# A list-scheduled attention-plus-MLP kernel: an order found by a search over its planner's keys, a warm-up on a constant, and an earlier release of one weight load

## Chip, cores, metric

The kernel runs on one core of a Trainium2 chip. The metric is the device time in microseconds (us) of one execution; medians of several executions are given. The span in a profile is about 1.7 us shorter than the time. All runs told here were in the fast state. By the 2% rule every kernel in this document is "the same" as the one before; what is compared below lies under 2%, and the 95% intervals say which of it is clear of the scatter.

## The reference, cut to what matters

```python
x = A_x                                             # 2048 x 512
g = sigmoid((x * gate_w).sum(-1))                   # one gate per row
a = A(x)   # q, k, v = x wq, x wk, x wv; 32 heads of 16; 4 segments of 512 rows:
           # o = gb * (phi(q) M) / (phi(q) z + 1e-6) + (1 - gb) * softmax(q k^T / 4 + mask) v
           # M += phi(k)^T v ; z += sum phi(k)    (after each segment);  a = o wo
b = B(x)   # h = relu(x W_gate) * (x W_up)  (1792 wide);  b = h W_down
out = g * a + (1 - g) * b                           # bf16
```

## The kernel before

The kernel doesn't fix an order by hand. It lists 1346 operations, each with the engines that can run it, a length in us, a key and what it depends on. A planner in the kernel then goes through simulated time and takes, on each engine, the ready operation with the lowest key. The result is the order in which all instructions are emitted. On the chip each engine is handed its own instructions in that order. Where an operand isn't there yet, the engine waits with it: at 105 us of the changed kernel, shown below, VectorE stands for 2.23 us before an operation although the operand of the next one has been ready for 1.4 us.

```python
MM, SW, MG = 0.216, 0.1, 1.0      # a dense matmul of 512 columns, a change of shape, a margin
...
    def run(self):                # in Sched
        ...
                    def pk(x):    # TensorE's choice: the key, and a bonus for staying in shape
                        t, o = x
                        k = o.key
                        if o.mode == "P":
                            k += -20.0 if mode == "R" else 4.0
                        elif o.mode == "D" and mode == "C" and "C" not in o.flex:
                            k += 3.0
                        return (k, o.seq)
        ...
            if e == "PE":
                o.ran = mode if mode in o.flex else o.mode
                if o.ran != mode:
                    dur += SW
                    mode = o.ran
```

The four shapes: D dense 128x128, C column strips 128x32, R the logits (four row strips of 32), P probabilities times values (64x32). The start, where x, wq and wk are loaded:

```python
    def c_zero(e):
        nc.vector.memset(zero[:, 0:P], 1.0)              # operand of the warm-up
    def c_dummy(e):
        for _ in range(28):                              # TensorE warm-up
            nc.tensor.matmul(g_dummy.t[:, 0:P], lhsT=zero[:, 0:P], rhs=zero[:, 0:P], ...)
    ...
    # x of segment 0 in four pieces by the SP and ACT queues; wq in three pieces by GpSimd's queue:
            nc.gpsimd.dma_start(out=wq_sb[:, c0:c1, :], in_=A_wq[c0 * P:c1 * P, :]...)
    ...
    lw["wk"] = loadw("wk", wk_sb, A_wk, 0, D, 1)         # by the SP queue; wv, wg, wu ... behind it
    o_wk0 = op("wk0", {"DVE": 0.08}, lambda e: nc.vector.memset(wk_sb[0:1, 0, 0:1], 0.0), key=-490, cls=0)
    lw["wk"].deps.append((o_wk0, None))
    ...
    o_wk0.deps.append((xc0[0][0], None))                 # after the first copy of x
```

The memset of one element of wk_sb is there only so that the load of wk has to wait for it. In the body, three things matter later: VectorE empties the PSUM of k and v (PSUM holds the buffers that TensorE writes its results to), it multiplies RG out of R, which GpSimd copies together, and it transposes output tiles that GpSimd has summed.

```python
            nc.gpsimd.tensor_copy(R[s][32 * j:32 * j + 32, k, :], rcol[32 * k:32 * k + 32, cols])  # 16 a segment
            nc.vector.tensor_tensor(RG[s % 2]..., HG..., rv..., ALU.mult)             # op RG{s}, waits for all R
            (nc.vector if e == "DVE" else nc.gpsimd).tensor_tensor(Oa.t[:], Oa.t[:], Ob.t[:], ALU.add)  # ad{s}{c}
            nc.vector.transpose(dst.t[:], Oa.t[:]...)                                 # ot{s}{c}, waits for ad
```

Of the kernel before, what the change touches and what calls it, by code (L numbers as in the profile page):

```python
# [7 lines left out]
BF16 = mybir.dt.bfloat16  # L8
F32 = mybir.dt.float32
ACT = mybir.ActivationFunctionType  # L10
ALU = mybir.AluOpType

P = 128
# [12 lines left out]
VW = H * HP + 16  # L26
VSW = H // 2 * HP + 16

MM = 0.216
SW = 0.1  # L30
MG = 1.0



# [20 lines left out]
class Sched:  # L55
# [5 lines left out]
    def op(self, name, engs, emit, deps=(), key=0.0, cls=1, mode=None, alloc=(), uses=(), land=0.0, flex=""):  # L61
        o = Op()
        o.flex, o.ran = flex, mode
        o.name, o.engs, o.emit, o.key, o.cls, o.mode = name, engs, emit, key, cls, mode
        o.alloc, o.uses = list(alloc), list(alloc) + list(uses)
        o.deps = [d if isinstance(d, tuple) else (d, None) for d in deps]
        o.deps = [d for d in o.deps if d[0] is not None]
        o.start = o.end = o.eng = None
        o.land = land
        o.succ, o.seq = [], len(self.ops)  # L70
        for b in o.uses:
            b.left += 1
        self.ops.append(o)
        return o
# [92 lines left out]
def kernel(  # L167
# [15 lines left out]
    nc = tc.nc  # L183
# [6 lines left out]
    def tl(name, shape, dt=BF16):  # L190
        return sb.tile(list(shape), dt, name=name)
# [9 lines left out]
    wq_sb, wk_sb, wv_sb, wo_sb = (tl(n, [P, NC, D]) for n in ("wq_sb", "wk_sb", "wv_sb", "wo_sb"))  # L201
# [1 line left out]
    ident = tl("ident", [P, P])  # L203
    mcol = tl("mcol", [P, 1], F32)
    mcole = tl("mcole", [P, 1], F32)
    scratch = tl("scratch", [P, 1], F32)
    bdm = tl("bdm", [P, 8, DH], F32)
    mzacc = tl("mzacc", [P, NC, 2 * (DH + 1)], F32)
    M2 = [tl(f"M2_{i}", [P, NC, 8, DH]) for i in range(2)]
# [13 lines left out]
    Op_ = pool("O", 4, [P, 16, 2, DH])  # L223
    oTp = pool("oT", 8, [P, L])
    osp = rgp = pool("os", 4, [P, D])
    zero = osp.tiles[0]
    smp = pool("sm", 3, [P, 2, 16], F32)
    zg, zc, rcol, rp1, ngcol = (tl(n, [P, NT], F32) for n in ("zg", "zc", "rcol", "rp1", "ngcol"))
    R = [tl(f"R{s}", [P, 4, 4], F32) for s in range(NSEG)]
# [8 lines left out]
    sc = Sched()  # L238
    op = sc.op
# [9 lines left out]
    ACTC = lambda n: 0.19 + 0.000833 * n  # L249


    def c_zero(e):
        nc.vector.memset(zero[:, 0:P], 1.0)  # L253
    o_zero = op("zero", {"DVE": 0.15}, c_zero, cls=0, key=-100)

    def c_ident(e):
        nc.gpsimd.memset(ident[:], 0.0)
# [2 lines left out]
    o_ident = op("ident", {"POOL": 0.6}, c_ident, cls=0, key=-100)  # L260

    def c_warm(e):
        nc.scalar.activation(scratch[:], zero[:, 0:1], ACT.Exp)
    o_warm = op("warm", {"ACT": 1.5}, c_warm, deps=[o_zero], cls=0, key=-100)

    def c_mcol(e):
# [20 lines left out]
    o_bdm = op("bdm", {"POOL": 1.5}, c_bdm, deps=[o_ident, o_vones], key=-10)  # L287

    def c_dummy(e):
        for _ in range(28):  # L290
            nc.tensor.matmul(g_dummy.t[:, 0:P], lhsT=zero[:, 0:P], rhs=zero[:, 0:P], start=True, stop=True)  # L291
    g_dummy = Buf(G)
    o_dummy = op("dummy", {"PE": 3.0}, c_dummy, deps=[o_zero], key=-1000, mode="D", alloc=[g_dummy])

# [18 lines left out]
    for i in range(2):  # L313
        for eng, q, h in (("SP", nc.sync, 0), ("ACT", nc.scalar, 1)):
            def f(e, i=i, q=q, h=h):
                q.dma_start(out=xn[0].t[:, 2 * h:2 * h + 2, 256 * i:256 * i + 256],
                            in_=x[256 * h:256 * h + 256, 256 * i:256 * i + 256].rearrange("(t p) d -> p t d", p=P))
            lx0[i, h] = load(f"x0_{i}{h}", f, 131072, -300 + i, eng=eng, alloc=[xn[0]] if (i, h) == (0, 0) else [],
                             uses=[] if (i, h) == (0, 0) else [xn[0]])
# [12 lines left out]
        return load(name, f, P * tile_.shape[1] * (c1 - c0) * 2, key, eng=eng)  # L332

    lw["wk"] = loadw("wk", wk_sb, A_wk, 0, D, 1)
    o_wk0 = op("wk0", {"DVE": 0.08}, lambda e: nc.vector.memset(wk_sb[0:1, 0, 0:1], 0.0), key=-490, cls=0)
    lw["wk"].deps.append((o_wk0, None))
    lw["wv"] = loadw("wv", wv_sb, A_wv, 0, D, 1)

# [59 lines left out]
    qS = Buf(Spool)  # L398
# [3 lines left out]
    first_x(1, None)  # L402
    for ci in range(NC):
        def f(e, ci=ci):
            for c in range(NC):
                nc.tensor.matmul(qS.t[:, c, :], lhsT=wq_sb[:, ci, c * P:(c + 1) * P], rhs=xT[0].t[:, ci, :],  # L406
                                 start=(ci == 0), stop=(ci == NC - 1))
        o_q0 = op(f"q0.{ci}", {"PE": 4 * MM * (1.5 if ci < 2 else 1)}, f,
                  deps=xc0[ci] + lwq[ci] + [(o_q0, 0.0) if ci else None],
                  key=-400 + ci, mode="D", alloc=[qS] + q0 if ci == 0 else [], uses=([] if ci == 0 else [qS]) + [xT[0]])  # L410
        if ci < 2:
            first_x(ci + 2, o_q0)
# [193 lines left out]
    def mz_mm(s, g):  # L606
        for c in range(NC):
            for t in range(4):
                for j in range(4):
                    h = 8 * c + 2 * j  # L610
                    nc.tensor.matmul(g.t[32 * j:32 * j + 32, W2 * c:W2 * c + W2],  # L611
                                     lhsT=pK[s].t[:, t, c * P + 32 * j:c * P + 32 * j + 32],
                                     rhs=Vp[s].t[:, t, h * HP:(h + 2) * HP].rearrange("p (h v) -> p h v", v=HP)[:, :, 0:DH + 1],
                                     start=(t == 0), stop=(t == 3), tile_position=(0, 32 * j))

    def mz_deps(s):
        return [o_pKt[s, c] for c in range(NC)] + [o_v[s, t] for t in range(4)]
# [21 lines left out]
    def mz0():  # L639
        g = Buf(G)  # L640
        k = dkey(3)
        a = op("mz0", {"PE": 0.5}, lambda e: mz_mm(0, g), deps=mz_deps(0), key=k, mode="C", alloc=[g], uses=[pK[0], Vp[0]])
        mz_after(0, a, g, k)


# [69 lines left out]
    rec_of = {}  # L715
# [4 lines left out]
    def unit(i):  # L720
        s, c = units[i]
        base = TA0 + (i // 2) * 2 * PU
        odd = i % 2
        FL = [[(c, 0, 0, 512)], [(c, 1, 0, 448), (c, 7, 448, 64)], [(c, 2, 0, 384), (c, 6, 384, 128)],
              [(c, 3, 0, 320), (c, 5, 320, 192)]]
        if not odd:
            FL.append([(c, 4, 0, 256), (c + 1, 4, 256, 256)])
        E, masks = {}, []
        for n, parts in enumerate(FL):
            sp, eb_ = Buf(Spool), Buf(Ep)  # L730
            kf = base + (n + 5 * odd) * 2 * PU / 9
            chunks = sorted({p[0] for p in parts})

            def f(e, parts=parts, sp=sp):
                for cc, kb, off, w in parts:
                    for j in range(4):
                        rows = slice(32 * j, 32 * j + 32)
                        nc.tensor.matmul(sp.t[:, j, off:off + w],  # L738
                                         lhsT=K2[s, cc].t[rows, kb, :, :].rearrange("p r k -> p (r k)"),
                                         rhs=QT[s, cc].t[rows, L - w:L], start=True, stop=True,  # L740
                                         tile_position=(32 * j, 0))
            a = op(f"f{s}{c}.{n}", {"PE": MM}, f,
                   deps=[o_q[s, cc] for cc in chunks] + [o for cc in chunks for o in o_k2[s, cc]] +
                   ([(fill_prev[0], 0.0)] if fill_prev[0] else []),
                   key=kf, mode="R", alloc=[sp], uses=[b_ for cc in chunks for b_ in (QT[s, cc], K2[s, cc])])
            fill_prev[0] = a
            if n == 1 and pending[0] is not None:
                rest(*pending[0], a)
                pending[0] = None

            def f(e, sp=sp, eb_=eb_):
                nc.scalar.activation(eb_.t[:], sp.t[:], ACT.Exp, scale=SCALE)  # L752
            b = op(f"e{s}{c}.{n}", {"ACT": 1.88}, f, deps=[a], key=kf, cls=0, alloc=[eb_], uses=[sp])
            offs = [p[2] for p in parts]

            def f(e, eb_=eb_, offs=offs):
                for off in offs:
                    for r in range(2):
                        v = eb_.t[64 * r:64 * r + 64, :, off:off + 64]
                        nc.gpsimd.affine_select(out=v, in_=v, compare_op=ALU.is_ge, fill=0.0, base=0,  # L760
                                                pattern=[[0, 4], [1, 64]], channel_multiplier=-1)
            m = op(f"m{s}{c}.{n}", {"POOL": 0.95 * len(parts)}, f, deps=[b], key=kf, uses=[eb_])
            for cc, kb, off, w in parts:
                if cc == c:
                    E[kb] = (eb_, off)
                else:
                    shared[s, cc] = (eb_, off, m)
            masks.append(m)
        if odd:
            E[4] = shared[s, c][0:2]  # L770
            masks.append(shared[s, c][2])
        pending[0] = (i, E, masks)
        if i == len(units) - 1:
            rest(i, E, masks, None)
# [4 lines left out]
    def dens(s, k0, org):  # L779
# [11 lines left out]
        rec_of[s, "den"] = rec_of[s, "mz"] = a  # L791
        if mds:
            gm = Buf(G)
            rec_of[s, "mz"] = am = op(f"mz{s}", {"PE": 0.5}, lambda e: mz_mm(s, gm), deps=[(a, 0.0)], key=k0 - 20, mode="C",
                                      alloc=[gm], uses=[pK[s], Vp[s]])
            gate_mz.append((s, am, gm, k0))
        T = Buf(Tp)
# [33 lines left out]
    def rest(i, E, masks, behind):  # L831
# [4 lines left out]
        def f(e):  # L836
            for kb in range(8):
                src, off = E[kb]
                w = L - 64 * kb
                for r in range(2):  # L840
                    rows = slice(64 * r, 64 * r + 64)
                    for j in range(4):
# [3 lines left out]
                        else:  # L846
# [1 line left out]
                            v = VS[s].t[rows, kb // 2, h * HP:h * HP + 32]  # L848
                        nc.tensor.matmul(gs[r].t[32 * j:32 * j + 32, L - w:L], lhsT=v, rhs=src.t[rows, j, off:off + w],  # L849
                                         start=(kb == 0), stop=(kb == 7), tile_position=(64 * r, 32 * j))  # L850
        a = op(f"pv{s}{c}", {"PE": 1.05}, f,
               deps=[(m, MG) for m in masks] + [o_v[s, t] for t in range(4)] + [o for t in range(4) for o in o_vs[s, t]] +
               ([(behind, 0.0)] if behind else []),
               key=k0 - 100, mode="P", alloc=gs, uses=list({id(v[0]): v[0] for v in E.values()}.values()) + [Vp[s], VS[s]])
# [128 lines left out]
    for t in range(4):  # L983
        dn(NSEG - 1, t)

    order = sc.run()
    if SIM_HOOK is not None:
        SIM_HOOK(sc)
# [36 lines left out]
```

## Time and profile before

| | before |
|---|---|
| time, median of 3 | 267.07 us (266.61 to 267.48) |
| TensorE busy | 97% of a span of 265.3 us |
| first q matmul, first k matmul | 5.19 us, 9.60 us |
| changes of TensorE's shape after 9 us | 170, 95.6 ns each |
| end of the last matmul, tail after it | 262.13 us, 3.14 us |

A line of the timeline is: start, length, engine, line of the program, operation, out<-in, shapes, how many were merged, and in brackets the idle time before and what ended it. The prediction below shows the lines. "Body" is used here for the time from the start of the first k matmul to the end of the last matmul: 252.53 us. The same matmuls lie between these two points in all of the kernels compared here.

### The profile page before, as it was taken

To read this page: it belongs to the slowest core of one execution; us is meant where nothing else is said; L and a number is where in the kernel's file an instruction comes from. 1 tells how busy PE (TensorE), PEld (TensorE's weight loads), DVE (VectorE), ACT (ScalarE), POOL (GpSimd) and SP (SyncE) were. 2 spreads that over 40 slices of the span, in tenths; PEclk is the share of its full clock that TensorE was granted. 3 is DMA by queue.
4 is the path that set the end of the run, shared out by engine and by line. 5 is a ranking of instruction groups with operands and counts; after the bars stand their busy time and mean duration, and the time that the engine had idled before them with its cause. 6 is when DMAs were issued, how large, how long until landed. Compare 5 with 4: busy or idle time off the path is not lost.

```text
span 265.3 us, 7048 instructions
## 1 busy us (share of the span) xinstructions
PE 257.0 (97%) x2808; PEld 115.9 (44%) x2844; DVE 183.8 (69%) x407; ACT 193.9 (73%) x189; POOL 191.0 (72%) x470
## 2 busy tenths in 40 slices
PE   8999999999999999999999999999999999999995
PEld 6433444444454444444434434344443444344444
DVE  1497888888975285998888837688985735566611
ACT  3598999899885558999896668898788566777010
POOL 8678888888559788798648988887878866537000
PEclk9999999999999999999999999999999999999999
DMA  5997990017310100000551010000000010000011
GB/s 162 289 252 203 313 261 13 4 40 80 100 26 1 42 20 22 0 2 2 132 88 23 21 42 20 4 2 0 2 0 4 0 42 23 20 2 0 2 41 40
DMA packets 27057, 15.54 MB, mean 59 GB/s; under 512 B 13584, under 2 KB 26896, under 8 KB 27024
## 3 DMA queue, kind: packets, MB, share of 16 engines
q1 hardware_dynamic: 26304, 14.30, 22.0%
q0 software_dynamic: 176, 0.52, 0.6%
q8 instruction: 22, 0.36, 0.6%
q10 hardware_dynamic: 544, 0.26, 0.3%
q14 instruction: 11, 0.09, 0.1%
HBM read 9.84 MB, written 2.10 MB: 45 GB/s over the span
## 4 chain that ended last, share of the span: by engine, by line
PE 97%; issue 2%; DVE 0%; ACT 0%; DVEq 0%
PE G L248 74%; PE S L738 9%; PE G L849 7%; PE G L246 3%; PE S L406 2%; PE G L291 1%; PE G L611 1%; PE G L785 0%; PE G L385 0%; DVE os L700 0%; ACT xT L395 0%; DVE os L253 0%; DVE mcole L268 0%; DVEq L700 0%; DVE mcol L267 0%
## 5 line engine op out<-in xcount | busy, mean ns | idle before, releaser
L752 ACT ACTIVATE E<-S 128x2048 bf16<-128x2048 f32 x72 | 135.1, 1876 | 34.3 <-PE S L738 31.9
L760 POOL TENSOR_SCALAR_AFFINE_SELECT E<-E 64x256 bf16<-64x256 bf16 x256 | 115.7, 452 | 38.5 <-ACT E L752 24.6
L248 PE MATMUL G<-xT,wu_sb 128*128 128x512 bf16 x211 | 57.3, 380 | 0.4 <-issue 0.2
L248 PE MATMUL G<-xT,wg_sb 128*128 128x512 bf16 x206 | 56.2, 380 | 1.1 <-issue 0.8
L663 DVE TENSOR_TENSOR hT<-G,os 128x512 bf16<-128x512 f32 x56 | 38.2, 684 | 19.7 <-ACT os L659 10.7
L248 PE MATMUL G<-wd_sb,hT 128*128 128x512 bf16 (+1 forms) x212 | 48.9, 365 | 1.1 <-issue 1.0
L884 DVE STREAM_TRANSPOSE T<-G 128x512 f32<-128x512 f32 x44 | 30.3, 702 | 14.0 <-PE G L849 8.2
L659 ACT ACTIVATE os<-G 128x512 bf16<-128x512 f32 x56 | 32.7, 597 | 6.1 <-PE G L248 5.3
L248 PEld LDWEIGHTS <-wu_sb 128*128 128x128 bf16 x218 | 19.9, 98 | 24.8 <-issue 3.0
L248 PEld LDWEIGHTS <-wg_sb 128*128 128x128 bf16 x218 | 19.4, 98 | 24.6 <-issue 4.1
L248 PEld LDWEIGHTS <-hT 128*128 128x128 bf16 x222 | 20.3, 98 | 22.3 <-issue 2.6
L738 PE MATMUL S<-QT,K 32*128 32x192 bf16 (+7 forms) x512 | 28.6, 287 | 0.5
L738 PEld LDWEIGHTS <-K 32*128 32x128 bf16 x512 | 8.2, 92 | 30.4 <-issue 29.9
L700 DVE TENSOR_SCALAR os<-G,ngcol 128x512 bf16<-128x512 f32 (+1 forms) x10 | 7.0, 697 | 19.4 <-PE G L248 19.3
L849 PE MATMUL G<-E,Vp 64*32 64x128 bf16 (+7 forms) x512 | 19.0, 284 | 0.2 <-issue 0.2
L849 PE MATMUL G<-E,VS 64*32 64x128 bf16 (+7 forms) x512 | 18.4, 284 | 0.0
L248 PE MATMUL G<-wo_sb,oT 128*128 128x512 bf16 (+1 forms) x66 | 17.2, 367 | 0.3 <-issue 0.3
L597 POOL COPY VS<-Vp 64x256 bf16<-64x256 bf16 x32 | 13.3, 416 | 4.8 <-DVE Vp L515 3.3
L904 DVE TENSOR_TENSOR O<-T,sm 128x256 bf16<-128x256 f32 x32 | 15.8, 524 | 0.3
L248 PE MATMUL G<-xT,wk_sb 128*128 128x512 bf16 x60 | 15.8, 380 | 0.3 <-issue 0.2
L702 ACT ACTIVATE os<-G,ngcol 128x512 bf16<-128x512 f32 x7 | 4.8, 687 | 15.0 <-PE G L248 15.0
L479 POOL COPY R<-rcol 32x4 f32<-32x4 f32 x64 | 13.5, 210 | 3.0
(98 smaller groups left out, 302.0 us busy)
## 6 DMA issues: line engine op xcount, KB each, us to landing
out_dram<-os SPq DMA_DIRECT2D x15, 128.0 KB, 1.7
wd_sb<-in_B_W_down_dram SPq DMA_DIRECT2D x1, 1792.0 KB, 13.4
xn<-in_A_x_dram SPq DMA_DIRECT2D x3, 512.0 KB, 4.7
wg_sb<-in_B_W_gate_dram SPq DMA_DIRECT2D x2, 512.0 KB, 5.8
wu_sb<-in_B_W_up_dram SPq DMA_DIRECT2D x2, 512.0 KB, 6.9
wg_sb<-in_B_W_gate_dram SPq DMA_DIRECT2D x3, 256.0 KB, 6.9
wu_sb<-in_B_W_up_dram SPq DMA_DIRECT2D x3, 256.0 KB, 7.2
wk_sb<-in_A_wk_dram SPq DMA_DIRECT2D x1, 512.0 KB, 4.0
```

The source lines that it names most:

```text
L246: nc.tensor.matmul(out_ap[q], lhsT=lhsT[:, q], rhs=rhs, start=start, stop=stop, tile_position=(0, 32 * j))
L248: nc.tensor.matmul(out_ap, lhsT=lhsT, rhs=rhs, start=start, stop=stop)
L479: nc.gpsimd.tensor_copy(R[s][32 * j:32 * j + 32, k, :], rcol[32 * k:32 * k + 32, cols])
L597: nc.gpsimd.tensor_copy(VS[s].t[64 * r:64 * r + 64, t, 0:H // 2 * HP].rearrange("p (h v) -> p h v", v=HP)[:, :, 0:DH], src[:, :, r, 0:DH])
L659: nc.scalar.activation(rg.t[:], g.t[:], ACT.Relu)
L663: nc.vector.tensor_tensor(h.t[:], u.t[:], rg.t[:], ALU.mult)
L738: nc.tensor.matmul(sp.t[:, j, off:off + w], lhsT=K2[s, cc].t[rows, kb, :, :].rearrange("p r k -> p (r k)"), rhs=QT[s, cc].t[rows, L - w:L] ...
L752: nc.scalar.activation(eb_.t[:], sp.t[:], ACT.Exp, scale=SCALE)
L760: nc.gpsimd.affine_select(out=v, in_=v, compare_op=ALU.is_ge, fill=0.0, base=0, pattern=[[0, 4], [1, 64]], channel_multiplier=-1)
L849: nc.tensor.matmul(gs[r].t[32 * j:32 * j + 32, L - w:L], lhsT=v, rhs=src.t[rows, j, off:off + w], start=(kb == 0), stop=(kb == 7), tile_po ...
L884: nc.vector.transpose(T.t[:].rearrange("p b e -> p (b e)"), g.t[:])
L904: nc.vector.tensor_tensor(O.t[:, :, r, :], T.t[:, :, 0:DH], sm.t[:, r, :, None].to_broadcast([P, 16, DH]), ALU.mult)
```

## The change

The intent: a search over the planner's keys, with lengths corrected from measurements, looks for an order that ends sooner; the warm-up no longer waits for VectorE; wk comes sooner.

```diff
-MM = 0.216
-SW = 0.1
+MM = 0.2159
+SW = 0.094
+NUDGE = { "f13.3": 24, "q12/0": -7, "g0.0/1": 81, ... }        # 64 entries, cut
...
-    def c_zero(e):
-        nc.vector.memset(zero[:, 0:P], 1.0)
+    ones = nc.const_aps.tensor(1.0, [P, P], BF16)
...
-        nc.scalar.activation(scratch[:], zero[:, 0:1], ACT.Exp)
+        nc.scalar.activation(wk_sb[:, 0, 0:1], ones[:, 0:1], ACT.Exp)
...
-        for _ in range(28):
-            nc.tensor.matmul(g_dummy.t[:, 0:P], lhsT=zero[:, 0:P], rhs=zero[:, 0:P], start=True, stop=True)
+        for _ in range(31):
+            nc.tensor.matmul(g_dummy.t[:, 0:P], lhsT=ones, rhs=ones, start=True, stop=True)
...
-    o_wk0 = op("wk0", {"DVE": 0.08}, lambda e: nc.vector.memset(wk_sb[0:1, 0, 0:1], 0.0), key=-490, cls=0)
+    o_wk0 = op("wk0", {"DVE": 0.08}, lambda e: None, key=-490, cls=0)
...
+            if ci == 0:                                   # ahead of the first q group
+                for _ in range(2):
+                    nc.tensor.matmul(qS.t[:, 0, 0:P], lhsT=ones, rhs=ones, start=True, stop=True)
...
-        a = op("mz0", {"PE": 0.5}, ...                    # also mz{s}
+        a = op("mz0", {"PE": 0.56}, ...
-            a = op(f"f{s}{c}.{n}", {"PE": MM}, f,         # logits
+            a = op(f"f{s}{c}.{n}", {"PE": 0.229}, f,
-        a = op(f"pv{s}{c}", {"PE": 1.05}, f,              # probabilities times values
+        a = op(f"pv{s}{c}", {"PE": 1.015}, f,
...
+    for o in sc.ops:
+        o.key += NUDGE.get(o.name, 0)
     order = sc.run()
```

Note that the planner still counts the load of wk as held by the first copy of x (the operation wk0 stays in the plan); only on the chip is it released sooner, by ScalarE's warm-up, which now writes into wk_sb.

> **What bounds the kernel now.** I read the page's head first (busy shares and the 40 slices), then the waits of TensorE, then TensorE's timeline at the start and in the middle, last the end of the run.
>
> ```profile
> PE 257.0 (97%) x2808; PEld 115.9 (44%) x2844; DVE 183.8 (69%) x407; ACT 193.9 (73%) x189; POOL 191.0 (72%) x470
> ...
> PE   8999999999999999999999999999999999999995
> ...
> PE 97%; issue 2%; DVE 0%; ACT 0%; DVEq 0%
> ```
>
> TensorE is busy in 97% of the span, and 97% of the chain that ended last is TensorE itself. Its busy share alone would not prove a bound, because the ends of matmuls are modelled. So the question is whether it ever waits. The waits of TensorE over the whole span:
>
> ```profile
> PE G L248 <- issue: 2.4, 15, 0.2
> PE G L291 <- DVE mcole L268: 1.1, 1, 1.1
> PE G L849 <- issue: 0.2, 1, 0.2
> ```
>
> No wait for ScalarE, VectorE, GpSimd or a DMA is left, but for the one at 0 us for the warm-up's operand. The page shows "issue" gaps of at most 0.2 us, where 2808 matmuls stand against 2844 weight loads: 36 matmul records are missing, and a missing record looks like a gap of one matmul. To be sure I took the starts of all matmul records in order. Of the 795 places after 9.6 us where one 128x128 matmul follows another, none starts over 14 ns later than its predecessor's columns allow (512 columns: 216 ns from start to start; 256: 109), missing records taken as one more step of 216 ns. From 5.185 us to 262.13 us TensorE does not stand still for anything but its own changes of shape. Those can be read in the timeline of TensorE:
>
> ```profile
> 63.25 1.03 PE L248 MATMUL G<-xT,wu_sb 128*128 128x512 bf16 x4
> 64.21 0.40 PE L738 MATMUL S<-QT,K 32*128 32x384 bf16 x8
> 64.54 1.04 PE L248 MATMUL G<-xT,wg_sb 128*128 128x512 bf16 x4
> 65.41 1.03 PE L248 MATMUL G<-xT,wu_sb 128*128 128x512 bf16 x4
> ```
>
> Four dense matmuls at 216 ns from 63.25 would be over at 64.11, but the logits (four row strips at once) start at 64.21: 0.10 us lost. A dense group beside a dense group loses nothing (64.54 to 65.41 is 0.87, four times 216). Leaving the logits costs the same again. Over the records in order, from 9.6 us on, I count 170 changes between the four shapes (dense 128x128, column strips 128x32, logits 32x128, probabilities times values 64x32). Their excess over the streaming time sums to 16.25 us, 95.6 ns each. That is all the body (252.5 us, 9.60 to 262.13) contains besides streaming.
>
> The start, same view:
>
> ```profile
> 1.12 3.17 PE L291 MATMUL G<-os 128*128 128x128 bf16 x28 [1.12 <-DVE mcole L268]
> 4.08 1.06 PE L385 MATMUL G<-ident,xn 128*128 128x128 bf16 x8
> 5.18 1.54 PE L406 MATMUL S<-xT,wq_sb 128*128 128x512 bf16 x4
> 6.56 0.39 PE L385 MATMUL G<-ident,xn 128*128 128x128 bf16 x4
> 6.79 1.03 PE L406 MATMUL S<-xT,wq_sb 128*128 128x512 bf16 x4
> 7.65 0.39 PE L385 MATMUL G<-ident,xn 128*128 128x128 bf16 x4
> 7.87 1.89 PE L406 MATMUL S<-xT,wq_sb 128*128 128x512 bf16 x7
> 9.60 0.59 PE L248 MATMUL G<-xT,wk_sb 128*128 128x512 bf16 x2
> ```
>
> The 28 warm-up matmuls run at 106.7 ns from start to start until 4.08, the first eight transposes of x follow without a gap until 4.93, then TensorE waits 0.26 us for the copies of x. The first projection matmuls take 378, 427 and 356 ns, the fourth 217: the clock is released at about 6.27. After that q runs on into k at 9.60 with no gap (seven records for eight matmuls, 7.87 + 8 x 0.216 = 9.60).
>
> The end: the last matmul is over at 262.13, VectorE scales 128x256 in 0.48 us, and the last store carries the span to 265.27, so 3.1 us of tail.
>
> **What the Trainium skill says.** "TensorE: Matmul & The Clock Gate", Part 1, says that the clock is halved until about 3.4 us of sustained activity, that the window is free-running, and that the point of release therefore varies from run to run. The trace agrees with halving (107 then 56 ns for 128 columns, 427 then 216 for 512); release comes 5.2 us after the first warm-up matmul, which a free window of 3.4 us allows (anything from 3.4 to 6.8). The same page, "Back-to-back issue gap", gives N/2.4 + 2.5 ns warm for a single matmul, 216 for 512 columns, and a lower sustained figure of 131; this trace never goes below 215, so 216 is the floor that I use. "TensorEngine Tiling (Array Packing)", Key Properties, says that changing the tiling mode drains TensorE; the trace puts 96 ns on it. "Trainium Kernel Development and Optimization", Key Constraints, says that DMAs issued from SP, ACT and POOL share the same 16 DMA engines and interleave; that bears on wk below, and the trace of before has wk alone after the first x and most of wq, so it does not show it.
>
> **The change part by part.**
>
> Order: no matmul is added or removed but five small ones at the start (below). In a body without stalls an order can only remove changes of shape. How many can go? The 72 logit groups share one PSUM buffer, and each is emptied by an exponential of 1.88 us, so two cannot stand beside each other: 72 entries and 72 exits stay. The 16 probabilities-times-values groups cost one change more if they follow a logit group and two if they stand among dense work; the records show 8 of each kind. Two of the five column-strip stretches are entered from dense work. So at most 8 + 2 = 10 of 170 changes can be saved, 10 x 95.6 ns = 0.96 us. The new model prices a change at 0.094 us, near the 95.6 ns measured, so the search can see this gain. But a group may follow its logits only if its masks are ready by then, so I expect it to get about half: -0.5 us. That the logits count 0.229 rather than 0.216 and the value group 1.015 rather than 1.05 makes the plan truer, but there is no wait in the trace that a truer plan could remove.
>
> Warm-up: the constant is written by the first memsets (0.38 to 0.48 in the timeline) and not by VectorE's at 0.89 to 1.06, so TensorE can start at some 0.87 instead of 1.12. 31 matmuls x 106.7 ns = 3.31 us end at 4.18, where before 28 ended at 4.08. x landed by about 3.97 (the first transpose's weight load starts then), so the transposes move by about +0.10 us. The two extra matmuls ahead of the first q fill 0.21 of the 0.26 us in which TensorE waits for the copies; they delay nothing. One pair of transposes moves ahead of its partner, so ScalarE's copy (0.38 us) can start before VectorE's (0.29), worth some 0.05. The first q: about +0.05 us. Against that, activity begins 0.25 us sooner, so on average the clock is released 0.25 us sooner, worth half of it in work done at double rate: -0.12. Together about -0.1 us.
>
> wk: VectorE's memset of one element, ended at 5.26, held the load of wk; now ScalarE's warm-up (ends 3.35) holds it. The load is issued at about 3.4 instead of 5.31, and everything behind it in the SP queue moves by 1.9 us. The first k matmul starts at 9.60 directly on the last q, so nothing waited for wk: gain 0. Its packets then share the DMA engines with wq, of which some 400 of 512 KB were still to come at 4.0; wq lands before 6 now and its last half is needed at 7.87, so 1.9 us of slack covers a slowdown: cost 0.
>
> Tail: unchanged if the halved tile is still the last. Some moves delay parts of the last segment's output tiles; if a full tile came last, its scaling is 0.75 instead of 0.48 and its store 1.7 instead of 1.5 us: +0.5. I give that a third: +0.15.
>
> Sum: -0.5 - 0.1 + 0 + 0.15 = -0.45. Since the order was chosen by a search that has the whole makespan as its measure, I trust it somewhat more than that and go to -0.85: 267.07 - 0.85 = 266.2.
>
> **The rivals.** First, a new stall takes the place of the changes saved: 64 shifted operations move loads, copies and masks too, and the plan's margins are small. For it: ScalarE, POOL and VectorE are each 69 to 73% busy, with slices at 9. Against: the old order held without one stall on an older, rougher price list. It would make 267.5 to 268.5. Second, the clock gate decides: a window that closes earlier spares the first q matmuls their half speed; at best the release falls before 5.18 and saves (378 + 427 + 356) - 3 x 216 = 513 ns, plus a little in the transposes; at worst it comes 1 us later and costs 0.5. The three times of before spread over 0.87 us, which such a free-running window would do. So 265.6 to 266.7. Third, wk's earlier packets push wq past its need, and q stalls; against it the 1.9 us of slack, for it that wq goes by another queue at a low rate. It would cost 0.5 to 1 us: 267. Fourth, the constant's operand has no real columns (one column read 128 times); if its weight load were slow, 31 matmuls would last twice as long, +3.3 us, 269.5. Nothing in the trace speaks for it.
>
> **Range and chances.** A gain of over 2% needs 5.3 us; the bounds above (0.96 of changes, about 0.6 of clock, no stall to remove) sum to under 1.6. A loss of 2% needs several new stalls or the slow constant. Spread: the order's gain 0 to 0.96, the clock ±0.5, the tail 0 to 0.5, repeatability ±0.3. I predict 266.2 us, 265.3 to 267.1 eight times in ten; faster by over 2% 0.02, within 2% 0.96, slower 0.02.
>
> **What would show it.** Right: TensorE's warm-up starts near 0.87 with no wait on VectorE; the wk load is issued near 3.4; k follows q without a gap; the waits of TensorE still name only "issue"; the changes of shape count 160 to 167 instead of 170; the last matmul ends 0.4 to 1 us earlier. Wrong: a wait of TensorE on ScalarE, POOL, VectorE or a load in the list of waits; more than 170 changes; a first q matmul later than 5.4; a tail over 3.3 us; or a body that shrinks by more than 1 us, which would mean that streaming time itself could be saved and the floor of 216 ns was not one.

## The result, and the profile after

The changed kernel took 267.46 us (median of 4, 267.38 to 267.70) beside 266.95 (median of 4, 266.61 to 267.48) before. The ratio is 1.0019, with a 95% interval of 1.0000 to 1.0037. Ratios in this document are the mean time of one kernel's fast runs over that of the other's of the same rounds, so not quite the ratio of the medians quoted. By the 2% rule it is the same; the forecast gain of 0.85 us did not come, and the time lies above the range.

The page of the changed kernel, the head of the chain that ended last:

```profile
PE 85%; POOL 6%; DMA 5%; issue 1%; DVE 1%; SPq 0%; POOLq 0%; DVEq 0%
PE G L259 66%; PE S L751 8%; PE G L862 6%; PE G L257 4%; DMA wu_sb<-in_B_W_up_dram 3%; POOL E L773 3%; DMA wq_sb<-in_A_wq_dram 2%; POOL R L492 1%; POOL CM L836 1%; PE S L419 1%; PE G L624 1%; POOL O L939 1%; POOL wq_sb L332 0%; PE G L798 0%; DVE oT L946 0%
```

Before, the chain was 97% TensorE. Now it runs through GpSimd (POOL), wq and a piece of wu. The waits of TensorE (us in total, times, longest) say where it is held:

```profile
...
PE S L419 <- DMA wq_sb<-in_A_wq_dram: 0.5, 1, 0.5
PE G L259 <- DVE KT L528: 0.4, 1, 0.4
PE G L259 <- DVE Vp L528: 0.4, 1, 0.4
```

The modelled end of a matmul hides some 0.16 us of each such wait: the record of a 512-column matmul lasts 379 ns, and the next one starts after 216. So I give the waits below as the distance from start to start less what the columns, and a change of shape if there is one, take. The start of the changed kernel in TensorE's timeline:

```profile
5.20 1.47 PE L419 MATMUL S<-xT,wq_sb 128*128 128x512 bf16 x4
...
7.59 0.39 PE L395 MATMUL G<-ident,xn 128*128 128x128 bf16 x4
8.46 1.90 PE L419 MATMUL S<-xT,wq_sb 128*128 128x512 bf16 x8 [0.48 <-DMA wq_sb<-in_A_wq_dram]
10.19 1.03 PE L259 MATMUL G<-xT,wk_sb 128*128 128x512 bf16 x4
```

The last transpose of x starts at 7.761 and takes 56 ns, so the third q group could start at 7.82. It starts at 8.46, 0.64 us late, when the last half of wq is there. The first k matmul is at 10.19 instead of 9.60.

The body, TensorE, VectorE and GpSimd around 105 us, in one timeline:

```profile
103.78 1.89 PE L259 MATMUL G<-wv_sb,xT 128*128 128x512 bf16 x8
104.17 0.86 POOL L492 COPY R<-rcol 32x4 f32<-32x4 f32 x4
105.07 0.38 DVE L497 TENSOR_TENSOR RG<-HG,R 128x128 f32<-128x128 f32 x1 [2.23 <-POOL R L492]
105.12 1.35 POOL L939 TENSOR_TENSOR O<-O,O 128x512 bf16<-128x512 bf16 x1
105.36 0.69 DVE L528 CAST KT<-G 128x512 bf16<-128x512 f32 x1
...
106.10 1.02 PE L259 MATMUL G<-wv_sb,xT 128*128 128x512 bf16 x4 [0.44 <-DVE KT L528]
...
106.50 0.71 DVE L946 STREAM_TRANSPOSE oT<-O 128x512 bf16<-128x512 bf16 x1 [0.45 <-POOL O L939]
107.06 0.40 PE L751 MATMUL S<-QT,K 32*128 32x448 bf16 x8
107.14 1.85 DVE L528 CAST Vp<-G 128x512 bf16<-128x512 f32 x3
...
107.85 1.02 PE L259 MATMUL G<-wv_sb,xT 128*128 128x512 bf16 x4 [0.39 <-DVE Vp L528]
```

This is one cause seen twice. GpSimd is late with the copies of R. VectorE's next operation in its order, RG, needs them, and VectorE stands for 2.23 us, although k's last matmul ended at 103.94 and its result could have been emptied 1.4 us before 105.36, when VectorE came to it. TensorE then lacks a free PSUM buffer and waits 0.60 us, until VectorE has emptied k. The same follows with GpSimd's sum, VectorE's transposition and v: 0.45 us.

The sum, from the starts of all matmul records:

| us | before | changed | difference |
|---|---|---|---|
| first k matmul | 9.60 | 10.19 | +0.59 |
| changes of shape in the body | 170, together 16.25 | 162, together 15.28 | -0.97 |
| other waits in the body | 0.34 | 0.25 + 0.60 + 0.45 + 0.11 = 1.41 | +1.07 |
| tail after the last matmul | 3.14 | 3.13 | -0.01 |
| sum | | | +0.68 |
| span | 265.27 | 265.97 | +0.70 |

The 0.34 us before is a pause inside one group of shape P at 45.7 us that the prediction overlooked. It stands in all five profiles without the shifted keys (0.27 to 0.39 us) and in none with them; its cause was not sought. The waits of 0.25 and 0.11 in the changed kernel are for a piece of wu at 47.9 us, which the new order issues at 40.8 instead of 23.7, and at 179.4 us.

### The profile page after: what moved, and what is told of

It is laid out like the page before. It is cut to its first block, busy times and chain, and to the rows that moved or that the text cites. A ratio compares the mean times of both kernels' runs of the same rounds, so it can differ in the third digit from the quotient of the medians.

```text
span 266.0 us, 7198 instructions
## 1 busy us (share of the span) xinstructions
PE 260.6 (98%) x2891; PEld 116.7 (44%) x2891; DVE 183.5 (69%) x407; ACT 193.4 (73%) x187; POOL 191.6 (72%) x470
## 4 chain that ended last, share of the span: by engine, by line
PE 85%; POOL 6%; DMA 5%; issue 1%; DVE 1%; SPq 0%; POOLq 0%; DVEq 0%
PE G L259 66%; PE S L751 8%; PE G L862 6%; PE G L257 4%; DMA wu_sb<-in_B_W_up_dram 3%; POOL E L773 3%; DMA wq_sb<-in_A_wq_dram 2%; POOL R L492 1%; POOL CM L836 1%; PE S L419 1%; PE G L624 1%; POOL O L939 1%; POOL wq_sb L332 0%; PE G L798 0%; DVE oT L946 0%
## 5 line engine op out<-in xcount | busy, mean ns | idle before, releaser
L773 POOL TENSOR_SCALAR_AFFINE_SELECT E<-E 64x256 bf16<-64x256 bf16 x256 | 114.1, 446 | 40.4 <-ACT E L765 23.1
L259 PE MATMUL G<-xT,wg_sb 128*128 128x512 bf16 x204 | 54.5, 380 | 0.0
L259 PE MATMUL G<-wd_sb,hT 128*128 128x512 bf16 (+1 forms) x238 | 54.4, 367 | 0.0
L259 PE MATMUL G<-xT,wu_sb 128*128 128x512 bf16 x200 | 53.0, 380 | 0.1
L259 PEld LDWEIGHTS <-hT 128*128 128x128 bf16 x238 | 22.0, 98 | 24.2 <-issue 2.6
L259 PEld LDWEIGHTS <-wu_sb 128*128 128x128 bf16 x200 | 18.3, 98 | 23.6 <-issue 3.0
L715 ACT ACTIVATE os<-G,ngcol 128x512 bf16<-128x512 f32 x10 | 6.9, 687 | 16.3 <-PE G L259 16.3
L610 POOL COPY VS<-Vp 64x256 bf16<-64x256 bf16 x32 | 14.3, 446 | 6.1 <-ACT Vp L530 3.3
L259 PE MATMUL G<-wv_sb,xT 128*128 128x512 bf16 x64 | 16.0, 379 | 0.8 <-DVE KT L528 0.4
L939 POOL TENSOR_TENSOR O<-O,O 128x512 bf16<-128x512 bf16 x11 | 13.2, 1199 | 2.9 <-DVE O L917 2.2
```

What stands on the lines that cost most here:

```text
L259: nc.tensor.matmul(out_ap, lhsT=lhsT, rhs=rhs, start=start, stop=stop)
L610: nc.gpsimd.tensor_copy(VS[s].t[64 * r:64 * r + 64, t, 0:H // 2 * HP].rearrange("p (h v) -> p h v", v=HP)[:, :, 0:DH], src[:, :, r, 0:DH])
L773: nc.gpsimd.affine_select(out=v, in_=v, compare_op=ALU.is_ge, fill=0.0, base=0, pattern=[[0, 4], [1, 64]], channel_multiplier=-1)
```

## The experiments

Theory A: the early wk costs the 0.6 us at the start, because its packets delay wq; the new order saves its 1.0 us but brings waits for VectorE that eat it. The rivals are named in each expectation. All runs had five rounds; the runs of one group share the chip and the runs of the kernel before (medians 267.08, 266.82 and 266.98 in the three groups). All results were correct. "First k", "body" and the clock's release are from each kernel's profiled run.

### Group 1: take the parts apart

**e1_gate.** The changed kernel with the old hold on wk.

```diff
-    o_wk0 = op("wk0", {"DVE": 0.08}, lambda e: None, key=-490, cls=0)
+    o_wk0 = op("wk0", {"DVE": 0.08}, lambda e: nc.vector.memset(wk_sb[0:1, 0, 0:1], 0.0), key=-490, cls=0)
```

> The changed kernel with VectorE's one-element memset of wk_sb put back, so that the load of wk is again held until the first copy of x (near 5.3 us); order and warm-up as in the change. Theory A (the early wk packets delay wq, and the second and later q matmuls wait 0.65 us for wq; the order's own stalls of about 1.4 us eat the 1.0 us that fewer changes of shape save): no wait of TensorE on wq, first k matmul at about 9.55 us instead of 10.19, time 0.6 us under the changed kernel, that is 266.8, and within 0.3 us of before. Rival B (wq's lateness is chance of the software queue and has nothing to do with wk): first k near 10.2 again in this run or in any, time as the changed kernel, 267.4.

Measured: 266.77 us, ratio 0.9987 (0.9971 to 1.0002). TensorE's waits in it:

```profile
...
PE G L259 <- DVE KT L528: 0.4, 1, 0.4
PE G L259 <- DVE Vp L528: 0.4, 1, 0.4
PE G L259 <- DMA wk_sb<-in_A_wk_dram: 0.3, 1, 0.3
```

The wait for wq is gone, as A says; first k is at 9.49. A new one is there: in this run the clock was released early, q was over at 9.00, and then TensorE waited 0.49 us for wk itself. So the old hold has a price as well, when the clock is early. The two waits on VectorE stay (0.59 and 0.45).

**e2_early.** The kernel before with only the early release of wk.

```diff
-        nc.scalar.activation(scratch[:], zero[:, 0:1], ACT.Exp)
+        nc.scalar.activation(wk_sb[:, 0, 0:1], zero[:, 0:1], ACT.Exp)
...
-    o_wk0 = op(..., lambda e: nc.vector.memset(wk_sb[0:1, 0, 0:1], 0.0), ...)
+    o_wk0 = op(..., lambda e: None, ...)
```

> The kernel before with one thing of the change: the load of wk held by ScalarE's warm-up activation (which now writes into wk_sb) and not by VectorE's memset, so that it is issued near 3.4 us. Order and warm-up operand as before. Theory A: TensorE waits 0.5 to 0.7 us for wq before the third q group, first k at about 10.2 instead of 9.60, time +0.6, that is 267.5. Rival B: first k at 9.6, time as before, 266.9.

Measured: 267.51 us, ratio 1.0027 (1.0005 to 1.0048). First k at 10.23. TensorE in the timeline (PEld is its loading of weights):

```profile
8.06 0.39 PE L385 MATMUL G<-ident,xn 128*128 128x128 bf16 x4
8.49 1.41 PEld L406 LDWEIGHTS <-wq_sb 128*128 128x128 bf16 x8 [0.22 <-DMA wq_sb<-in_A_wq_dram]
8.50 1.90 PE L406 MATMUL S<-xT,wq_sb 128*128 128x512 bf16 x8
10.23 2.10 PE L248 MATMUL G<-xT,wk_sb 128*128 128x512 bf16 x9
```

The third q group starts at 8.50, though the transposes end at 8.29: 0.21 us late. This wait is smaller than A expected, because in this run the clock came late (7.11 us) and TensorE reached this place late anyway. What A says of the first k, 10.2, is what came, but in part by luck: without the wait it would have been 10.02 in this run. Rival B, chance, falls all the same: every profile with wk early and wq by GpSimd's queue has the wait (0.21 to 1.56 us from start to start), and none with the old hold has it there.

**e3_order.** The kernel before with the new keys and lengths alone (the lengths, as in the change, are left out below); the order of all operations is the changed kernel's.

```diff
+    for o in sc.ops:
+        o.key += NUDGE.get(o.name, 0)
     order = sc.run()
```

> The kernel before with the order of the change alone (its shifted keys and its lengths; the order of all operations is the same as the changed kernel's), start as before. Theory A: 162 changes of shape instead of 170 (saves 1.0 us), new waits of TensorE for VectorE at about 105 and 107 us and for a late weight piece at about 48, 1.0 to 1.4 us together; first k at 9.6; time within 0.4 us of before. Rival C (the waits in the changed kernel's body come from its later start and its shifted loads, not from the order): no wait in the body, time 0.9 us under before, 266.0.

Measured: 267.01 us, ratio 1.0001 (0.9984 to 1.0017). 162 changes of shape, waits of 0.56 and 0.45 us at 104.1 and 106.1 us, body 252.31. The wait near 48 us, for the piece of wu, did not come in this run or in any later one, so that 0.25 us was chance. Rival C falls: the waits come with the order. First k at 9.29, with a wait for the first piece of wq and 0.30 us for wk; the clock was released at 3.85 us here.

**e4_start.** The changed start with the order and lengths of before.

```diff
-NUDGE = { "f13.3": 24, ... }
+NUDGE = {}          # and MM, SW, logits, values, sums as before
```

> The changed kernel's start (constant warm-up, wk released early) with the order and lengths of before. Theory A: a wait for wq as in the changed kernel, first k at about 10.2, no waits in the body, time 0.6 us over before, 267.5, equal to the changed kernel within 0.3. Rival C: as before, 266.9, since the start by itself costs nothing and the order makes all of the difference.

Measured: 267.98 us, ratio 1.0039 (1.0020 to 1.0058), 0.5 us more than expected. First k at 10.32 after a wait for wq of 1.22 us from start to start. The body is 252.96, not 252.5: a wait of 0.38 us for VectorE at 139 us came on top. Rival C falls here too.

### Group 2: take the causes away

**f1_gate_body.** The gated kernel (that of e1_gate) with two of VectorE's operations moved back in the found order.

```diff
     order = sc.run()
+    for name, behind in (("RG2", "ve21"), ("ot10", "ve21")):
+        o = next(o for o in order if o.name == name)
+        order.remove(o)
+        order.insert(next(i for i, q in enumerate(order) if q.name == behind) + 1, o)
```

> The gated kernel of the first experiment, with two VectorE operations of the found order put a few places later in VectorE's own order: the product RG of segment 2 (which waits for GpSimd's copies of R) and the transposition of the first output tile of segment 1 (which waits for GpSimd's sum) now stand behind the emptying of k and of two v tiles. Theory A (GpSimd runs up to 3.4 us behind the plan there, and VectorE, which takes its work in order, holds back the PSUM emptying that TensorE needs): the waits of TensorE near 104 and 106 us (0.59 and 0.45 in the gated kernel) go, last matmul less first k is 251.4 instead of 252.39, time 0.9 us under the gated kernel, 265.9. Rival D (TensorE waits there because VectorE and the PSUM buffers are too slow for that stretch in any order): the waits move a little later, time as the gated kernel, 266.8.

Measured: 265.77 us, ratio 0.9958 (0.9943 to 0.9973). The timeline at the same place:

```profile
102.78 2.75 PE L259 MATMUL G<-wv_sb,xT 128*128 128x512 bf16 x12
102.98 0.69 DVE L528 CAST KT<-G 128x512 bf16<-128x512 f32 x1 [1.15 <-PE G L259]
103.16 0.85 POOL L492 COPY R<-rcol 32x4 f32<-32x4 f32 x4
103.85 0.69 DVE L528 CAST Vp<-G 128x512 bf16<-128x512 f32 x1 [0.17 <-PE G L259]
...
105.94 0.36 DVE L497 TENSOR_TENSOR RG<-HG,R 128x128 f32<-128x128 f32 x1
```

VectorE now empties k at once, 12 v matmuls run without a gap (before 8, a wait, then 4), GpSimd's last copies of R are as late as in e1_gate (2.4 us behind the plan in both), and RG waits for nothing. Body 251.32, 1.07 us less than in e1_gate, which is the two waits of 0.59 and 0.45 and a little of a third. Rival D falls: the same work is done in time once the two operations stand behind it. Two operations in other places bring as much as all the changes of shape that the search saved.

**f2_wqsp.** The changed kernel, wk early, with wq by the SP queue ahead of wk.

```diff
-            nc.gpsimd.dma_start(out=wq_sb[:, c0:c1, :], ...)
+            nc.sync.dma_start(out=wq_sb[:, c0:c1, :], ...)
```

> The changed kernel with its three loads of wq issued from the SP queue, behind the first x pieces and ahead of wk, instead of from GpSimd's queue; wk stays released early. Theory A (wk's packets delay wq because wq comes by another queue; in one queue wk cannot pass it): no wait for wq, first k between 9.0 and 9.6 as the clock's release falls, time 0.6 to 0.9 under the changed kernel, 266.7. Rival E (the DMA engines have too little room at the start for x, wq and wk together, by whatever queue): a wait for wq or wk of 0.5 us stays, time as the changed kernel, 267.4.

Measured: 266.73 us, ratio 0.9996 (0.9981 to 1.0011), by their medians 0.73 under the changed kernel (another group of runs). No wait for wq or wk, first k at 9.09, straight after q:

```profile
7.36 1.89 PE L419 MATMUL S<-xT,wq_sb 128*128 128x512 bf16 x8
9.09 1.89 PE L259 MATMUL G<-xT,wk_sb 128*128 128x512 bf16 x8
```

Rival E falls: the DMA engines have room for all three. But the edit does two things at once: wq leaves GpSimd's queue, and its last piece is issued by 3.21 us, before wk, where GpSimd's queue issued it until 3.91. Whether any second queue would be held up by wk, or only GpSimd's, was not tested; wq by the queue of ScalarE with wk early would tell.

**f3_wqsp_body.** Both together.

> Both of the above together, wq by the SP queue with wk early and the two VectorE operations moved. Theory A: the gains add, 1.6 us under the changed kernel, 265.8, 0.5% under before. If Rival D and E hold: 267.4.

Measured: 265.95 us, ratio 0.9960 (0.9944 to 0.9977). First k 9.31 with the clock released at 5.66, body 251.30. The gains add to within 0.15 us of the forecast. It is not better than f1_gate_body of the same rounds (265.77), although nothing waits for wk; the two differ by less than their scatter (265.2 to 266.1, and 265.4 to 266.0).

**f4_wqsp_old.** The changed start with wq by the SP queue, old order and lengths.

> The start of the change (constant, wk early) with wq by the SP queue, order and lengths of before. Theory A: no wait for wq; first k between 9.0 and 9.6; body as before 252.5; time 0.8 us under the kernel with the change's start and old order (267.98 measured), 0 to 0.4 us under before, 266.9. Rival E: 267.9.

Measured: 267.39 us, ratio 1.0016 (0.9999 to 1.0033), 0.5 above what was expected, 0.6 under e4_start. No wait for wq, but the third pair of transposes came at 6.55 (in e4_start at 6.06), waiting for a piece of x, one of which stands behind the first piece of wq in the queue in this edit (first k 9.73; f2_wqsp and f3_wqsp_body have the same queue and no such wait, so that cause is not shown), and the old order again had a wait of 0.34 us at 138.5. So wq no longer waits behind the early wk, but this start brings the old order no gain.

### Group 3: lengths, keys, and the moment of release

**g1_lengths** and **g2_nudge.** The gated kernel with the new lengths without the keys, and with the keys on the old lengths.

> The gated kernel (start of the change, wk held by VectorE's memset) with the new lengths but none of the shifted keys. The order that comes out has 171 changes of shape. Theory F (the search over keys saves the changes of shape, the lengths alone save none; the lengths take slack out of the plan, and GpSimd falls behind it): 171 changes, body (first k to end of the last matmul) 252.4 to 253.4 us, some wait of TensorE on VectorE in it, time 266.8 to 267.6. Rival G (the shifted keys alone bring the waits): no wait in the body, 252.4, time 266.6.

> The gated kernel with the shifted keys but the old lengths of logits, values, sums and changes of shape. The order that comes out has 164 changes. Theory F: more slack for GpSimd, waits of TensorE on VectorE in the body under 0.3 us, body 251.7 to 252.0, time 266.2. Rival G: waits of about 1 us as in the changed kernel, body 252.5, time 266.9.

Measured: lengths alone 267.21 us, ratio 1.0010 (0.9994 to 1.0025): 171 changes of shape, no wait on VectorE, body 252.50. Keys alone 266.65, ratio 0.9989 (0.9976 to 1.0002): 164 changes, body 252.37, and this wait of TensorE:

```profile
PE G L259 <- DVE KT L528: 0.7, 1, 0.7
```

From start to start it is 0.84 us, at 104.3 us. So my Theory F, that the truer lengths took the slack out of the plan, falls in the main: the lengths bring neither the saving nor the wait. The shifted keys bring both, as Rival G says, though it put the lengths alone at 266.6 and the keys alone at 266.9, and the measured times stand the other way round. And the wait of g2_nudge is only one of the two: VectorE stands there 1.96 us at the transposition, for GpSimd's sum, while the plan of that order puts RG behind the emptying of k and v, at 108.85 us. So that RG came to stand in front took keys and lengths together.

**g3_mid_body** and **g4_early_body.** The changed kernel with the two moves in VectorE's order; in g3 wk is held until GpSimd has issued the last of wq.

```diff
             nc.gpsimd.dma_start(out=wq_sb[:, c0:c1, :], ...)
+            if c0 == 2:
+                nc.gpsimd.memset(wk_sb[0:1, 0, 0:1], 0.0)
```

> The changed kernel with the two VectorE operations moved, and wk held by a one-element memset of GpSimd behind its last issue of wq, so that wk is issued near 4.0 us, between 3.4 (change) and 5.3 (before). Theory A (wk's packets stop those of wq that are still to come, so the later wk the less of wq is held up): wait for wq between 0 and 0.6 us, first k 9.2 to 9.9, time 265.6 to 266.2. Rival H (any wk issued before the last byte of wq costs the full delay): first k 10.1 or later, time 266.6.

> The changed kernel as it is (wk early, wq by GpSimd's queue) with only the two VectorE operations moved. Theory A: wait for wq as in the changed kernel, first k at 10.2, no wait on VectorE near 105 us, body 251.4; time 1.0 us under the changed kernel, 266.5, and 0.7 over the gated kernel with the same two moves (265.77 measured). Rival D: 267.4.

Measured: wk in between 265.17 us, ratio 0.9941 (0.9926 to 0.9956); wk early 266.32, ratio 0.9978 (0.9966 to 0.9990). The waits of g4_early_body name wq:

```profile
PE S L419 <- DMA wq_sb<-in_A_wq_dram: 1.4, 1, 1.4
```

In g3_mid_body, the SP queue's and TensorE's timelines:

```profile
4.01 0.37 SPq L343 DMA_DIRECT2D wk_sb<-in_A_wk_dram  x1
...
7.21 1.89 PE L421 MATMUL S<-xT,wq_sb 128*128 128x512 bf16 x8
8.94 1.89 PE L259 MATMUL G<-xT,wk_sb 128*128 128x512 bf16 x8
```

With wk issued at 4.01 there is no wait for wk and none for the last half of wq (the very first piece of wq held the weight load by 0.28 us, since TensorE, with an early clock, was there sooner), and first k comes at 8.94, the earliest of all. Both have the same body of 251.31 us. Rival H falls. This is the version that beats both kernels, by less than the 2% rule asks: by 0.6% the kernel before, and by 2.3 us the changed one (267.46 in an earlier group). Part of the 0.6 us over f1_gate_body (other rounds) is the clock: it was released at 4.25 us in this run.

## Why the prediction was wrong

It put 266.2 us, 265.3 to 267.1; measured were 267.46. Its bound, that the change lies within 2%, held. By its own steps:

**Order: the changes of shape.** Right, and undersized: half of the possible 0.96 us was expected, 162 changes are left (the text allowed 160 to 167) and 0.97 us went. The search found eight of the ten changes that could go, 0.76 us at 95.6 ns; the other 0.2 us is that the 162 left take 94.3 ns each. The experiments with lengths and keys apart show that the keys did it.

**Order: "no stall to remove", so none to fear.** This step failed. The count behind it looked only at places where one 128x128 matmul follows another, and so missed the pause of 0.34 us inside a group of shape P; the greater part of the error is what it left out. The sum gave new waits nothing and left them to the first rival; they measured 1.41 us in the profiled run, of which 1.05 came back in every profile of the changed order in which the two operations were not moved (1.04 in e1_gate, 1.01 in e3_order, 1.02 in f2_wqsp), and went in all four in which they were. The engine behind the wait was in the rival's list, but not the way: VectorE is only 69% busy, and it isn't too slow: with two operations moved (f1_gate_body) it does the same work without holding TensorE. The new order put an operation that needs GpSimd ahead of one that TensorE needs. The planner states a start for every operation, and GpSimd's 466 instructions can be set beside it in order: the last copies of R for segment 2 start 3.4 us after their planned time in the changed kernel; before, they started 0.1 us ahead of it. The plan of the change takes the copies to be over at 101.70 and places RG at 102.79, so that VectorE is free at 103.19 for k, planned at 103.51: 0.3 us to spare. The copies ended at 105.03, while TensorE itself was only 0.6 us behind its plan there. I left the question of margins at a sentence, although the change's own text names "measured lengths" and shows them for TensorE alone. Why GpSimd lags there is not settled: single instructions of one kind vary (a copy to CM takes 256 ns in the mean, at most 683; before 225, at most 731), and part of it is the later start.

**The lean of 0.4 us toward the search.** The working gave -0.45, and the prediction went on to -0.85 because a search had chosen the order. That had no number behind it. What the search improves is the plan: the planner's own end of the last matmul went from 262.91 to 260.18, 2.7 us, of which 1.1 is the new lengths alone (261.79 in the plan of g1_lengths); on the chip it went from 262.13 to 262.84.

**wk: "gain 0, cost 0".** The gain of 0 was right for the run that it was read from, where the clock came late; in four of the six profiles with the old hold, those with the clock earlier, k waited 0.2 to 0.5 us for wk. The cost failed: 0.64 us of waiting, the third rival. The prediction had the number that it needed, 1.9 us of slack for wq, and took it to be enough. The chain of the changed kernel's first 10 us shows the delay:

```profile
2.66 0.52 POOL wq_sb L332
3.18 5.23 DMA wq_sb<-in_A_wq_dram
```

The last load of wq, which took 3.3 us from issue to landing before, took 5.2. The DMA packets in the trace show when: from 5.5 to 6.5 us wk's queue moved 123 and 162 KB in the two half microseconds, and wq's queue 4 and 20; the rest of wq, some 240 KB, came from 6.5 to 8. Before, wq's queue moved 168 KB in the half microsecond from 5.0 and was done by 6. The Trainium skill, "DMA: Bandwidth & Descriptors", Queues, rings and completion order, says that each DMA engine takes turns between the queues that have work. By the trace's records the packets of wq are 4 KB and those of wk 1 KB, so turns of one packet each would have left wq the larger part of the bytes; it had under a tenth. Nor were the engines full all the time. In the half microsecond before, wq's queue had already dropped to 12 KB and wk's moved 12 KB too, with the 16 engines 38% busy (the last two figures of this line are that share and GB/s):

```profile
5.00:5.50 0.50, 0.50 (x5) 0.24 (x3) 0.27 (x2) 0.31 (x1) 0.50 (x1) 1.00 0.38 49
```

And in g3_mid_body, with wk issued behind the last of wq, the two queues did share: from 5.5 to 6.5 us 92 KB of wk and the last 80 of wq. So plain competition for room does not account for it. Whether wq's packets were ready to go in that time is not shown by the trace, and the mechanism below this stays open; that the early wk is the cause is shown by e1_gate and e2_early (one edit, both ways), and that wq in wk's own queue, ahead of it, does not suffer is shown by f2_wqsp.

The profiled runs fall in two clean sets: with wk early and wq by GpSimd's queue first k is at 10.19, 10.23, 10.32 and 10.59, with the clock's release at 6.13, 7.11, 5.03 and 4.05; with the old hold it is at 9.60, 9.49, 9.29, 9.45, 9.66 and 9.33. In the first set an earlier clock does not bring an earlier first k, because wq sets the end. It could explain the small scatter of the changed kernel's times (0.32 us, before 0.87), but e2_early and e4_start, with the same early wk, scatter by 1.3 us and more, so that isn't shown.

**Warm-up.** Right in its mechanism: it starts at 0.84 (predicted 0.87), the transposes at 4.10 (4.18), the first q at 5.20 (before 5.19, predicted +0.05), and the constant runs at the same 106.7 ns, so the fourth rival falls. Its worth of 0.1 us cannot be separated: e1_gate against e3_order, which differ in it alone, is 0.24 us by the medians in its favour, with overlapping ranges and the clock released at different times.

**Tail.** The fear of 0.15 us was idle: 3.13 us, as before.

**The clock.** The second rival's range was fair: in thirteen profiles that record it, the release falls between 3.85 and 7.11 us. The narrower range in the prediction's reading, 3.4 to 6.8 us after the first warm-up matmul, was an estimate from the page's window and does not hold: it came after 2.7 us in e3_order and after 3.2 in g4_early_body.

With both failed terms put in as measured, the prediction's own sum works: -0.97 + 1.07 + 0.59 - 0.01 = +0.68 in the profiled run. That is bookkeeping of one run; that the two terms are the causes rests on the experiments.

## What to carry to other kernels

When the bounding engine has no waits left, an order can only save its own switching costs, and any new wait is pure loss; so look in the new order for places where an engine has an operation that waits for a third engine in front of one that the bounding engine needs. A planner's gain is a gain of the plan: compare planned with measured starts of every engine, not only of the one whose lengths were corrected. A load that nothing waits for should not be issued ahead of another queue's load on the critical path: wk at 3.4 us, before GpSimd had issued the last of wq, cost 0.6 us, and at 4.0, just behind it, cost nothing, though wq was still in flight. Issue it behind that one, or put both in one queue.

## What the Trainium skill lacked or had wrong

- "DMA: Bandwidth & Descriptors", Queues, rings and completion order: the turns between queues that have work do not by themselves account for what was seen. While wk's queue (SP) moved 285 KB in 1 us, in packets of 1 KB, GpSimd's queue moved 24 KB of wq's remaining 260, in packets of 4 KB. The page names no reason why GpSimd's queue should all but stop when SP's starts. By one queue, in f2_wqsp, there was no delay.
- "TensorE: Matmul & The Clock Gate", Part 1, gives a scatter of about 500 ns either way for the clock's release. Here it fell between 3.85 and 7.11 us in profiles with nearly the same start, and once (3.85) only 2.7 us after the first warm-up matmul, less than the 3.4 that the prediction took from the page.
- The same page, Back-to-back issue gap, names 131 ns as the sustained distance for 512 columns; here it was never under 214 in any profile.
- "TensorEngine Tiling (Array Packing)", Key Properties, says that a change of the tiling mode drains TensorE but gives no figure: 96 ns at each of 170 changes.
